# SwiGLU feed-forward in bf16: x turned by DMAs in a written order, and the last output tile in column pieces of 256, 128 and 128

## The chip, the core and the metric

The kernel runs on one core of one Trainium2 chip. The metric is device microseconds of one execution, given as the median of several runs. Engines are named as in the profile: PE is TensorE's matmuls and PEld its weight loads, DVE is VectorE, ACT ScalarE, POOL GpSimd, and SP the engine whose queue issues every DMA here. SBUF is the on-chip memory of 128 partitions; PSUM is the memory of eight banks for each partition that TensorE writes into.

## What is computed

```python
B, S, D, F = 32, 32, 512, 1792        # x (B,S,D), w1 and w3 (D,F), w2 (F,D), all bf16

gate = jnp.einsum("bsd,df->bsf", x, w1)
up   = jnp.einsum("bsd,df->bsf", x, w3)
h    = silu(gate) * up                # silu(g) = g * sigmoid(g)
out  = jnp.einsum("bsf,fd->bsd", h, w2)
```

B and S are flattened into N = 1024 tokens.

## The kernel before

With 128 partitions P, D is DT = 4 tiles, F is FT = 14 feature tiles, and N is NT = 8 token tiles or two blocks of NB = 512 tokens. A matmul contracts over the partition dimension, so the first stage needs x with features on partitions: that is `xT`, shaped (128, 4, 1024). It comes into being in two steps. Two DMAs load x with tokens on partitions into `x_sb` (lines 64 and 81). `x_transposes` (line 98) then turns each 128x128 piece on TensorE against an identity (`ident`, line 53), four pieces into one PSUM tile `pT` (line 103), and copies that tile to `xT`: on VectorE for block 0 (line 109), on ScalarE for block 1 (line 111).

All DMAs are issued by SP, in the order of lines 64 to 85: the first half of x, w1 and w3 in chunks of 2, 2, 2, 4 and 4 feature tiles (with the second half of x after the fourth pair of chunks), then w2 in two halves. Nine matmuls on a zeroed tile `warm_sb` keep TensorE at work during the first loads (line 90); POOL zeroes that tile (line 52).

Then, for each block of 512 tokens and each feature tile `fo`, TensorE makes a gate tile (4 matmuls of 128x512, line 119) and an up tile (4 more, line 127) in PSUM, two buffers each. ScalarE takes the sigmoid of the gate (line 135), VectorE multiplies gate by sigmoid (line 139) and the product by up (line 140), and writes bf16 into `hT`, which again has features on partitions.

In the second stage each token tile accumulates 14 matmuls of 128x512 over the feature tiles into `o_ps` (line 148); ScalarE casts it to bf16 (line 159) and SP stores it (line 160). The last token tile is made in two pieces of 256 columns, 14 matmuls each, and VectorE casts them (line 157).

The order in which each engine executes is not the written one: the framework's scheduler decides it from its own estimate. So the transposes of block 1, which the program writes after all of block 0, stand on TensorE among block 0's matmuls. PSUM's eight banks hold two buffers of `pT`, two each of gate and up, and two of `o_ps`.

Of the kernel before, what the change touches and what calls it, by code (L numbers as in the profile page):

```python
# [1 line left out]

# [5 lines left out]


@with_exitstack
def kernel(
    ctx: ExitStack,
    tc: tile.TileContext,
    x: bass.AP,
    w1: bass.AP,
    w3: bass.AP,
    w2: bass.AP,
    out: bass.AP,
):  # L20
    nc = tc.nc
    P = nc.NUM_PARTITIONS
    fp32 = mybir.dt.float32
    bf16 = mybir.dt.bfloat16

    B, S, D = x.shape
    F = w1.shape[1]
    N = B * S
    assert D % P == 0 and F % P == 0 and N % P == 0
    DT = D // P  # L30
    FT = F // P
    NT = N // P
    NB = 512
    assert N % NB == 0 and NB % P == 0
    NBLK = N // NB
    NT_PER_BLK = NB // P

    x_flat = x.flatten_outer_dims()
    out_flat = out.flatten_outer_dims()
    x_view = x_flat.rearrange("(nt p) d -> p nt d", p=P)  # L40
    w1_v = w1.rearrange("(dt p) f -> p dt f", p=P)
    w3_v = w3.rearrange("(dt p) f -> p dt f", p=P)
    w2_v = w2.rearrange("(ft p) d -> p ft d", p=P)

    consts = ctx.enter_context(tc.tile_pool(name="consts", bufs=1))
    work = ctx.enter_context(tc.tile_pool(name="work", bufs=3))
    psum_t = ctx.enter_context(tc.tile_pool(name="psum_t", bufs=2, space=bass.MemoryType.PSUM))
    psum = ctx.enter_context(tc.tile_pool(name="psum", bufs=2, space=bass.MemoryType.PSUM))
    psum2 = ctx.enter_context(tc.tile_pool(name="psum2", bufs=2, space=bass.MemoryType.PSUM))

    warm_sb = consts.tile([P, NB], bf16, name="warm_sb")
    nc.gpsimd.memset(warm_sb[:], 0.0)  # L52
    ident = consts.tile([P, P], bf16, name="ident")
    make_identity(nc, ident[:])

    x_sb = consts.tile([P, NT, D], bf16, name="x_sb")
    xT = consts.tile([P, DT, N], bf16, name="xT")
    w1_sb = consts.tile([P, DT, F], bf16, name="w1_sb")
    w3_sb = consts.tile([P, DT, F], bf16, name="w3_sb")
    w2_sb = consts.tile([P, FT, D], bf16, name="w2_sb")  # L60
    hT = consts.tile([P, FT, N], bf16, name="hT")

    half = NT // 2
    nc.sync.dma_start(out=x_sb[:, 0:half, :], in_=x_view[:, 0:half, :])  # L64

    chunk_sizes = [2, 2, 2, 4, 4]
    bounds = []
    cb = 0
    for csz in chunk_sizes:
        ce = min(FT, cb + csz)  # L70
        if cb < ce:
            bounds.append((cb, ce))
        cb = ce
    assert cb >= FT, (cb, FT)

    for i, (cb0, cb1) in enumerate(bounds):
        f0, f1 = cb0 * P, cb1 * P
        nc.sync.dma_start(out=w1_sb[:, :, f0:f1], in_=w1_v[:, :, f0:f1])  # L78
        nc.sync.dma_start(out=w3_sb[:, :, f0:f1], in_=w3_v[:, :, f0:f1])  # L79
        if i == 3:  # L80
            nc.sync.dma_start(out=x_sb[:, half:NT, :], in_=x_view[:, half:NT, :])

    FH = FT // 2
    nc.sync.dma_start(out=w2_sb[:, 0:FH, :], in_=w2_v[:, 0:FH, :])
    nc.sync.dma_start(out=w2_sb[:, FH:FT, :], in_=w2_v[:, FH:FT, :])

    NWARM = 9
    warm_ps = psum_t.tile([P, NB], fp32, name="warm_ps", tag="tp")
    for i in range(NWARM):
        nc.tensor.matmul(  # L90
            warm_ps[:],
            lhsT=warm_sb[:, 0:P],
            rhs=warm_sb[:],
            start=True,
            stop=True,
        )

    def x_transposes(nb: int):
        for dt in range(DT):
            pT = psum_t.tile([P, NB], bf16, name="pT", tag="tp")  # L100
            for j in range(NT_PER_BLK):
                nt = nb * NT_PER_BLK + j
                nc.tensor.transpose(  # L103
                    pT[:, j * P : (j + 1) * P],
                    x_sb[:, nt, dt * P : (dt + 1) * P],
                    ident[:],
                )
            if nb == 0:
                nc.vector.tensor_copy(xT[:, dt, nb * NB : (nb + 1) * NB], pT[:])  # L109
            else:  # L110
                nc.scalar.copy(xT[:, dt, nb * NB : (nb + 1) * NB], pT[:])  # L111

    for nb in range(NBLK):
        x_transposes(nb)
        for fo in range(FT):
            gate_ps = psum.tile([P, NB], fp32, name="gate_ps")
            up_ps = psum.tile([P, NB], fp32, name="up_ps")
            for dt in range(DT):
                nc.tensor.matmul(  # L119
                    gate_ps[:],  # L120
                    lhsT=w1_sb[:, dt, fo * P : (fo + 1) * P],
                    rhs=xT[:, dt, nb * NB : (nb + 1) * NB],
                    start=(dt == 0),
                    stop=(dt == DT - 1),
                )
            for dt in range(DT):
                nc.tensor.matmul(  # L127
                    up_ps[:],
                    lhsT=w3_sb[:, dt, fo * P : (fo + 1) * P],
                    rhs=xT[:, dt, nb * NB : (nb + 1) * NB],  # L130
                    start=(dt == 0),
                    stop=(dt == DT - 1),
                )
            sig = work.tile([P, NB], fp32, name="sig")
            nc.scalar.activation(  # L135
                sig[:], gate_ps[:], mybir.ActivationFunctionType.Sigmoid
            )
            t = work.tile([P, NB], fp32, name="t")
            nc.vector.tensor_mul(t[:], gate_ps[:], sig[:])  # L139
            nc.vector.tensor_mul(hT[:, fo, nb * NB : (nb + 1) * NB], t[:], up_ps[:])  # L140

    for nt in range(NT):
        DB = 256 if nt == NT - 1 else 512
        assert D % DB == 0
        for db in range(D // DB):
            o_ps = psum2.tile([P, DB], fp32, name="o_ps", tag="o_ps")
            for fo in range(FT):
                nc.tensor.matmul(  # L148
                    o_ps[:],
                    lhsT=hT[:, fo, nt * P : (nt + 1) * P],  # L150
                    rhs=w2_sb[:, fo, db * DB : (db + 1) * DB],
                    start=(fo == 0),
                    stop=(fo == FT - 1),
                )
            o_sb = work.tile([P, DB], bf16, name="o_sb", tag="o_sb")
            if nt == NT - 1:
                nc.vector.tensor_copy(o_sb[:], o_ps[:])  # L157
            else:
                nc.scalar.copy(o_sb[:], o_ps[:])  # L159
            nc.sync.dma_start(  # L160
                out=out_flat[nt * P : (nt + 1) * P, db * DB : (db + 1) * DB],
                in_=o_sb[:],
            )


# [1 line left out]
_INS = ['x', 'w1', 'w3', 'w2']  # L167
_OUTS = [((32, 32, 512), 'bfloat16')]


# [23 lines left out]
```

## Time and profile before

| | |
|---|---|
| median of 13 runs | 92.55 us (91.28 to 93.02) |
| the profiled execution's own time | 91.86 us |
| its span, first to last instruction | 90.1 us |
| busy in the span: PE, PEld, DVE, ACT, POOL | 80.3, 37.7, 40.8, 24.2, 1.2 us |
| mean granted TensorE clock | 0.981 |
| moved by DMA | 7.67 MB, of which 1.05 MB written |

The span is what the trace covers; the execution's time is 1.76 us longer. TensorE's busy time is no measure of its load, since matmuls overlap; a start-to-start distance in a full stretch is. "L119" is line 119 above. In rows of the chain and the timeline the first number is the start in us, the second the length.

### The profile page before, as it was taken

The page shows a single profiled execution, that of the slowest core. Times are in us where ns is not written, and L with a number is a line of the kernel's source. Part 1 is how long each engine was busy: PE and PEld are TensorE (multiplying, and loading weights), DVE is VectorE, ACT ScalarE, POOL GpSimd, SP SyncE. Part 2 cuts the span into 40 slices and gives each one's busy share as a digit, 9 for nine tenths or more (in the row PEclk, how much of TensorE's full clock was granted, in tenths as well). Part 3 has the DMA queues.
Part 4 walks back from the last instruction along what each step waited for, and adds up shares of the span by engine and source line. Part 5 has one row for each costly group of instructions (what it writes and reads, how often), then busy time and mean ns, then how long its engine had stood idle before and what let it go on. Part 6 is the DMA issues. An engine that isn't in the chain of part 4 may idle for free.

```text
span 90.1 us, 1022 instructions
## 1 busy us (share of the span) xinstructions
PE 80.3 (89%) x384; PEld 37.7 (42%) x391; DVE 40.8 (45%) x62; ACT 24.2 (27%) x40; POOL 1.2 (1%) x7
## 2 busy tenths in 40 slices
PE   4989603999999999999999999999999999999960
PEld 1354202334444444454444444444444444444750
DVE  0045530338778887726887887877600000000030
ACT  5002200222342243575243234224022022202200
POOL 5000000000000000000000000000000000000000
PEclk9999999579999999999999999999999999999999
DMA  0999999997000000000000000000001110111021
GB/s 20 331 281 305 338 349 348 348 349 242 0 7 0 0 0 0 0 0 0 0 0 4 7 0 0 0 0 4 0 16 42 58 58 6 60 58 58 0 87 29
DMA packets 9461, 7.67 MB, mean 85 GB/s; under 512 B 368, under 2 KB 9456, under 8 KB 9456
## 3 DMA queue, kind: packets, MB, share of 16 engines
q1 hardware_dynamic: 9456, 7.60, 27.4%
q8 instruction: 3, 0.05, 0.2%
q14 instruction: 2, 0.02, 0.1%
HBM read 6.55 MB, written 1.05 MB: 84 GB/s over the span
## 4 chain that ended last, share of the span: by engine, by line
PE 78%; DMA 8%; SPq 7%; ACT 2%; issue 1%; DVE 0%; DVEq 0%
PE o_ps L148 26%; PE up_ps L127 26%; PE gate_ps L119 25%; DMA x_sb<-in_x_dram 8%; SPq L79 3%; SPq L78 3%; ACT xT L111 2%; SPq L64 0%; DVE o_sb L157 0%; PE pT L103 0%; DVEq L157 0%
## 5 line engine op out<-in xcount | busy, mean ns | idle before, releaser
L119 PE MATMUL gate_ps<-xT,w_sb 128*128 128x512 bf16 x109 | 29.8, 388 | 0.3 <-ACT xT L111 0.2
L127 PE MATMUL up_ps<-xT,w_sb 128*128 128x512 bf16 x110 | 29.5, 386 | 0.3 <-issue 0.2
L135 ACT ACTIVATE sig<-gate_ps 128x512 f32<-128x512 f32 x28 | 16.7, 597 | 41.9 <-PE gate_ps L119 40.7
L139 DVE TENSOR_TENSOR t<-gate_ps,sig 128x512 f32<-128x512 f32 x28 | 19.4, 691 | 15.0 <-ACT sig L135 14.8
L148 PE MATMUL o_ps<-w_sb,hT 128*128 128x512 bf16 (+1 forms) x124 | 24.4, 355 | 0.1
L140 DVE TENSOR_TENSOR hT<-t,up_ps 128x512 bf16<-128x512 f32 x28 | 19.2, 687 | 3.8 <-PE up_ps L127 1.2
L148 PEld LDWEIGHTS <-hT 128*128 128x128 bf16 x126 | 12.3, 98 | 11.9
L127 PEld LDWEIGHTS <-w_sb 128*128 128x128 bf16 x112 | 11.1, 99 | 14.4 <-issue 2.0
L119 PEld LDWEIGHTS <-w_sb 128*128 128x128 bf16 x112 | 11.0, 100 | 12.8 <-issue 0.8
L157 DVE CAST o_sb<-o_ps 128x256 bf16<-128x256 f32 x2 | 0.8, 424 | 22.2 <-PE o_ps L148 22.2
L159 ACT CAST o_sb<-o_ps 128x512 bf16<-128x512 f32 x7 | 4.1, 586 | 17.5 <-PE o_ps L148 15.1
L103 PE MATMUL pT<-ident,x_sb 128*128 128x128 bf16 x32 | 3.1, 226 | 4.7 <-DMA x_sb<-in_x_dram 4.4
L103 PEld LDWEIGHTS <-x_sb 128*128 128x128 bf16 x32 | 2.4, 103 | 6.8 <-DMA x_sb<-in_x_dram 4.9
L90 PE MATMUL warm_ps<-warm_sb 128*128 128x512 bf16 x9 | 4.0, 631 | 1.3 <-POOL warm_sb L52 1.3
L109 DVE COPY xT<-pT 128x512 bf16<-128x512 bf16 x4 | 1.6, 423 | 5.8 <-PE pT L103 5.7
L90 PEld LDWEIGHTS <-warm_sb 128*128 128x128 bf16 x9 | 1.2, 143 | 3.2 <-issue 1.9
L111 ACT COPY xT<-pT 128x512 bf16<-128x512 bf16 x4 | 2.1, 588 | 0.4 <-PE pT L103 0.4
L135 ACT ACT_TABLE_LOAD x1 | 1.3, 1283 | 0.7 <-PEq L178 0.7
L52 POOL MEMSET warm_sb<- 128x512 bf16 x1 | 0.5, 524 | 0.3 <-POOLq L178 0.3
masks.py:199 POOL TENSOR_SCALAR_AFFINE_SELECT ident<-ident 128x128 bf16<-128x128 bf16 x1 | 0.3, 292 | 0.1
masks.py:197 POOL MEMSET ident<- 128x128 bf16 x1 | 0.2, 205 | 0.0
L178 POOL MEMSET const-float32-0.0<- 128x1 f32 x1 | 0.1, 98 | 0.2 <-issue 0.2
(3 smaller groups left out, 0.3 us busy)
## 6 DMA issues: line engine op xcount, KB each, us to landing
w_sb<-in_w_dram SPq DMA_DIRECT2D x4, 512.0 KB, 7.2
w_sb<-in_w_dram SPq DMA_DIRECT2D x2, 896.0 KB, 10.4
w_sb<-in_w_dram SPq DMA_DIRECT2D x6, 256.0 KB, 5.5
x_sb<-in_x_dram SPq DMA_DIRECT2D x2, 512.0 KB, 5.5
out_dram<-o_sb SPq DMA_DIRECT2D x7, 128.0 KB, 1.7
out_dram<-o_sb SPq DMA_DIRECT2D x2, 64.0 KB, 1.5
```

Of the source, the lines that this page charges most:

```text
L78: nc.sync.dma_start(out=w1_sb[:, :, f0:f1], in_=w1_v[:, :, f0:f1])
L79: nc.sync.dma_start(out=w3_sb[:, :, f0:f1], in_=w3_v[:, :, f0:f1])
L90: nc.tensor.matmul(warm_ps[:], lhsT=warm_sb[:, 0:P], rhs=warm_sb[:], start=True, stop=True,)
L103: nc.tensor.transpose(pT[:, j * P : (j + 1) * P], x_sb[:, nt, dt * P : (dt + 1) * P], ident[:],)
L111: nc.scalar.copy(xT[:, dt, nb * NB : (nb + 1) * NB], pT[:])
L119: nc.tensor.matmul(gate_ps[:], lhsT=w1_sb[:, dt, fo * P : (fo + 1) * P], rhs=xT[:, dt, nb * NB : (nb + 1) * NB], start=(dt == 0), stop=(dt ...
L127: nc.tensor.matmul(up_ps[:], lhsT=w3_sb[:, dt, fo * P : (fo + 1) * P], rhs=xT[:, dt, nb * NB : (nb + 1) * NB], start=(dt == 0), stop=(dt = ...
L135: nc.scalar.activation(sig[:], gate_ps[:], mybir.ActivationFunctionType.Sigmoid)
L139: nc.vector.tensor_mul(t[:], gate_ps[:], sig[:])
L140: nc.vector.tensor_mul(hT[:, fo, nb * NB : (nb + 1) * NB], t[:], up_ps[:])
L148: nc.tensor.matmul(o_ps[:], lhsT=hT[:, fo, nt * P : (nt + 1) * P], rhs=w2_sb[:, fo, db * DB : (db + 1) * DB], start=(fo == 0), stop=(fo == ...
L159: nc.scalar.copy(o_sb[:], o_ps[:])
```

## The change

The changed kernel switches the scheduler off (`manual_schedule`), so every engine executes in the order written. x is turned on its way in: three transposing DMAs (`dma_start_transpose`) write `xT` straight from memory, tokens 0 to 255, 256 to 511 and 512 to 1023. `x_sb`, `ident`, `pT`, the 32 transposes and the eight copies are gone, and with them the two PSUM buffers of `pT`; gate and up have three buffers each. The warm-up matmuls read a constant 1.0, broadcast, that the framework sets up before the program starts, instead of a tile that POOL zeroes. Feature tiles 0 and 1 of block 0 are made together and in half-width matmuls (128x256): first both gates and both ups for tokens 0 to 255, then the same for tokens 256 to 511, then both SwiGLU groups. The last token tile of the output is made in pieces of 256, 128 and 128 columns.

```diff
-    psum_t = ctx.enter_context(tc.tile_pool(name="psum_t", bufs=2, space=bass.MemoryType.PSUM))
-    psum = ctx.enter_context(tc.tile_pool(name="psum", bufs=2, space=bass.MemoryType.PSUM))
-    psum2 = ctx.enter_context(tc.tile_pool(name="psum2", bufs=2, space=bass.MemoryType.PSUM))
+    psum_o = ctx.enter_context(tc.tile_pool(name="psum_o", bufs=2, space=bass.MemoryType.PSUM))
+    psum = ctx.enter_context(tc.tile_pool(name="psum", bufs=3, space=bass.MemoryType.PSUM))
 
-    warm_sb = consts.tile([P, NB], bf16, name="warm_sb")
-    nc.gpsimd.memset(warm_sb[:], 0.0)
-    ident = consts.tile([P, P], bf16, name="ident")
-    make_identity(nc, ident[:])
+    ctx.enter_context(tc.manual_schedule())
...
-    half = NT // 2
-    nc.sync.dma_start(out=x_sb[:, 0:half, :], in_=x_view[:, 0:half, :])
+    def load_x_transposed(n0, n1):
+        nc.sync.dma_start_transpose(out=xT[:, :, n0:n1], in_=x_flat[n0:n1, :])
...
-    for i, (cb0, cb1) in enumerate(bounds):
-        f0, f1 = cb0 * P, cb1 * P
-        nc.sync.dma_start(out=w1_sb[:, :, f0:f1], in_=w1_v[:, :, f0:f1])
-        nc.sync.dma_start(out=w3_sb[:, :, f0:f1], in_=w3_v[:, :, f0:f1])
-        if i == 3:
-            nc.sync.dma_start(out=x_sb[:, half:NT, :], in_=x_view[:, half:NT, :])
...
+    def load_w(c0, c1):
+        load_w1(c0, c1)
+        load_w3(c0, c1)
+
+    load_x_transposed(0, HB)
+    load_w(0, 2)
+    load_x_transposed(HB, NB)
+    load_w(2, 4)
+    load_w(4, 6)
+    load_x_transposed(NB, N)
+    load_w(6, 10)
+    load_w(10, FT)
...
+    one = nc.const_aps.tensor(1.0, [P, 1], bf16)
+    warm_ps = psum_o.tile([P, NB], fp32, name="warm_ps", tag="o_ps")
...
-            lhsT=warm_sb[:, 0:P],
-            rhs=warm_sb[:],
+            lhsT=one.to_broadcast([P, P]),
+            rhs=one.to_broadcast([P, NB]),
...
-    def x_transposes(nb: int):
+    def project(ps, w_sb, fo, n0, n1, c0):
...
-            pT = psum_t.tile([P, NB], bf16, name="pT", tag="tp")
-            for j in range(NT_PER_BLK):
-                nt = nb * NT_PER_BLK + j
-                nc.tensor.transpose(
-                    pT[:, j * P : (j + 1) * P],
-                    x_sb[:, nt, dt * P : (dt + 1) * P],
-                    ident[:],
-                )
-            if nb == 0:
-                nc.vector.tensor_copy(xT[:, dt, nb * NB : (nb + 1) * NB], pT[:])
-            else:
-                nc.scalar.copy(xT[:, dt, nb * NB : (nb + 1) * NB], pT[:])
+            nc.tensor.matmul(
+                ps[:, c0 : c0 + n1 - n0],
+                lhsT=w_sb[:, dt, fo * P : (fo + 1) * P],
+                rhs=xT[:, dt, n0:n1],
+                start=(dt == 0),
+                stop=(dt == DT - 1),
+            )
+
+    def gate_up_tiles():
+        gate_ps = psum.tile([P, NB], fp32, name="gate_ps")
+        up_ps = psum.tile([P, NB], fp32, name="up_ps")
+        return gate_ps, up_ps
+
+    def swiglu(gate_ps, up_ps, fo, nb):
+        sig = work.tile([P, NB], fp32, name="sig")
+        nc.scalar.activation(sig[:], gate_ps[:], SIGMOID)
+        t = work.tile([P, NB], fp32, name="t")
+        nc.vector.tensor_mul(t[:], gate_ps[:], sig[:])
+        nc.vector.tensor_mul(hT[:, fo, nb * NB : (nb + 1) * NB], t[:], up_ps[:])
+
+    g0, u0 = gate_up_tiles()
+    g1, u1 = gate_up_tiles()
+    project(g0, w1_sb, 0, 0, HB, 0)
+    project(g1, w1_sb, 1, 0, HB, 0)
+    project(u0, w3_sb, 0, 0, HB, 0)
+    project(u1, w3_sb, 1, 0, HB, 0)
+    project(g0, w1_sb, 0, HB, NB, HB)
+    project(g1, w1_sb, 1, HB, NB, HB)
+    project(u0, w3_sb, 0, HB, NB, HB)
+    project(u1, w3_sb, 1, HB, NB, HB)
+    swiglu(g0, u0, 0, 0)
+    swiglu(g1, u1, 1, 0)
 
     for nb in range(NBLK):
...
-        for fo in range(FT):
-            gate_ps = psum.tile([P, NB], fp32, name="gate_ps")
-            up_ps = psum.tile([P, NB], fp32, name="up_ps")
...
+        for fo in range(2 if nb == 0 else 0, FT):
+            gate_ps, up_ps = gate_up_tiles()
+            project(gate_ps, w1_sb, fo, nb * NB, (nb + 1) * NB, 0)
+            project(up_ps, w3_sb, fo, nb * NB, (nb + 1) * NB, 0)
+            swiglu(gate_ps, up_ps, fo, nb)
...
-        DB = 256 if nt == NT - 1 else 512
-        assert D % DB == 0
-        for db in range(D // DB):
-            o_ps = psum2.tile([P, DB], fp32, name="o_ps", tag="o_ps")
+        last = nt == NT - 1
+        c0 = 0
+        for DB in (D // 2, D // 4, D // 4) if last else (D,):
+            o_ps = psum_o.tile([P, DB], fp32, name="o_ps", tag="o_ps")
...
-                    rhs=w2_sb[:, fo, db * DB : (db + 1) * DB],
+                    rhs=w2_sb[:, fo, c0 : c0 + DB],
...
-            if nt == NT - 1:
+            if last:
...
-                out=out_flat[nt * P : (nt + 1) * P, db * DB : (db + 1) * DB],
+                out=out_flat[nt * P : (nt + 1) * P, c0 : c0 + DB],
...
+            c0 += DB
...
```

SP's list of loads moves with it. Before (tiles `x_sb`, `w1_sb`, `w3_sb`; the number is the buffer's; the shape is partitions x pieces x elements):

```order
L64 DMA x_sb_77<-in_x_dram 128x4x512
L78 DMA w1_sb_79<-in_w1_dram 128x4x256
L79 DMA w3_sb_80<-in_w3_dram 128x4x256
...
L78 DMA w1_sb_79<-in_w1_dram 128x4x512
L79 DMA w3_sb_80<-in_w3_dram 128x4x512
L81 DMA x_sb_77<-in_x_dram 128x4x512
```

And now, on the same engine (a row's wait names the completion count of one of eight DMA lanes, `DMAHW0` to `DMAHW7`, which the transfers take in turn):

```order
L57 DMA_TRANSPOSE xT_69<-in_x_dram 128x4x256
L60 DMA w1_sb_70<-in_w1_dram 128x4x256
L63 DMA w3_sb_71<-in_w3_dram 128x4x256
L57 DMA_TRANSPOSE xT_69<-in_x_dram 128x4x256
L60 DMA w1_sb_70<-in_w1_dram 128x4x256
L63 DMA w3_sb_71<-in_w3_dram 128x4x256
L60 DMA w1_sb_70<-in_w1_dram 128x4x256
L63 DMA w3_sb_71<-in_w3_dram 128x4x256
L57 DMA_TRANSPOSE xT_69<-in_x_dram 128x4x512 [waits DMAHW0_49]
L60 DMA w1_sb_70<-in_w1_dram 128x4x512 [waits DMAHW1_49]
```

The second half of x stood behind the weights of tiles 6 to 9; its transposing DMA now stands ahead of them, and the first half is split around the first pair of weights.

On TensorE, before, two transposes of block 1 stood between the up tile of feature tile 1 and the gate tile of feature tile 2 (`x_sb` is x as loaded, `ident` the identity):

```order
L127 MATMUL up_ps_147<-xT_78,w3_sb_80 128x512
L103 LDWEIGHTS x_sb_77 [waits DMAHW1_49]
L103 MATMUL pT_341<-ident_72,x_sb_77 128x128 [waits PE_49]
L103 LDWEIGHTS x_sb_77
L103 MATMUL pT_341<-ident_72,x_sb_77 128x128
L119 LDWEIGHTS w1_sb_79 [waits DMAHW3_49]
L119 MATMUL gate_ps_161<-xT_78,w1_sb_79 128x512 [waits DVE_49]
```

At the same place now, and at the start (rows between left out):

```order
L85 MATMUL warm_ps_89<-const-bfloat16-1.0 128x512
L95 LDWEIGHTS w1_sb_70 [waits DMAHW1_49]
L95 MATMUL gate_ps_99<-xT_69,w1_sb_70 128x256 [waits DMAHW0_49]
...
L95 LDWEIGHTS w3_sb_71 [waits DMAHW2_49]
...
L95 MATMUL gate_ps_99<-xT_69,w1_sb_70 128x256 [waits DMAHW3_49]
...
L95 MATMUL up_ps_102<-xT_69,w3_sb_71 128x256
L95 LDWEIGHTS w1_sb_70 [waits DMAHW4_49]
L95 MATMUL gate_ps_145<-xT_69,w1_sb_70 128x512
```

The transposes are gone from it, and the waits left are for x and weights in the order in which SP issues them: lanes 0, 1 and 2 at the start, lane 3 (the second quarter of x) between the two halves of the first pair, lane 4 ahead of feature tile 2.

More of the change, by code (lines that the diff above doesn't have):

```diff
@@ L28 @@
     N = B * S
-    assert D % P == 0 and F % P == 0 and N % P == 0
+    NB = 512
+    HB = NB // 2
     DT = D // P
@@ L32 @@
     NT = N // P
-    NB = 512
-    assert N % NB == 0 and NB % P == 0
     NBLK = N // NB
     NT_PER_BLK = NB // P
+    assert D % P == 0 and F % P == 0 and N % NB == 0
     x_flat = x.flatten_outer_dims()
     out_flat = out.flatten_outer_dims()
-    x_view = x_flat.rearrange("(nt p) d -> p nt d", p=P)
     w1_v = w1.rearrange("(dt p) f -> p dt f", p=P)
@@ L46 @@
     work = ctx.enter_context(tc.tile_pool(name="work", bufs=3))
-    psum_t = ctx.enter_context(tc.tile_pool(name="psum_t", bufs=2, space=bass.MemoryType.PSUM))
-    psum = ctx.enter_context(tc.tile_pool(name="psum", bufs=2, space=bass.MemoryType.PSUM))
-    psum2 = ctx.enter_context(tc.tile_pool(name="psum2", bufs=2, space=bass.MemoryType.PSUM))
-    warm_sb = consts.tile([P, NB], bf16, name="warm_sb")
-    nc.gpsimd.memset(warm_sb[:], 0.0)
-    ident = consts.tile([P, P], bf16, name="ident")
-    make_identity(nc, ident[:])
-    x_sb = consts.tile([P, NT, D], bf16, name="x_sb")
+    psum_o = ctx.enter_context(tc.tile_pool(name="psum_o", bufs=2, space=bass.MemoryType.PSUM))
+    psum = ctx.enter_context(tc.tile_pool(name="psum", bufs=3, space=bass.MemoryType.PSUM))
+    ctx.enter_context(tc.manual_schedule())
     xT = consts.tile([P, DT, N], bf16, name="xT")
@@ L85 @@
     nc.sync.dma_start(out=w2_sb[:, FH:FT, :], in_=w2_v[:, FH:FT, :])
+    one = nc.const_aps.tensor(1.0, [P, 1], bf16)
+    warm_ps = psum_o.tile([P, NB], fp32, name="warm_ps", tag="o_ps")
     NWARM = 9
-    warm_ps = psum_t.tile([P, NB], fp32, name="warm_ps", tag="tp")
     for i in range(NWARM):
@@ L113 @@
-    for nb in range(NBLK):
-        x_transposes(nb)
-        for fo in range(FT):
-            gate_ps = psum.tile([P, NB], fp32, name="gate_ps")
-            up_ps = psum.tile([P, NB], fp32, name="up_ps")
[L118 to L140, printed above, removed]
```

17 lines of the change are left out of this document (6 added, 11 removed).

## The prediction

> **What bounds the kernel now.** I read the page's head and its forty slices first, for where TensorE is not full.
>
> ```profile
> span 90.1 us, 1022 instructions
> PE   4989603999999999999999999999999999999960
> PEclk9999999579999999999999999999999999999999
> GB/s 20 331 281 305 338 349 348 348 349 242 0 7 0 0 0 0 0 0 0 0 0 4 7 0 0 0 0 4 0 16 42 58 58 6 60 58 58 0 87 29
> ```
>
> A slice is 2.25 us. PE is full from slice 8 to the last two, so the end is set by TensorE's own work; what is not work lies in the first 20 us, at one crossing in the middle, and in the tail. The hole at slices 4 to 6 falls where the DMA engines still run at 348 GB/s: it waits for a transfer. The granted clock halves just behind it. The chain of waits names the transfer:
>
> ```profile
> 7.46 7.39 DMA x_sb<-in_x_dram
> 14.85 0.05 issue
> 14.89 0.29 PE pT L103 x2
> 15.18 1.98 PE gate_ps L119 x6
> ```
>
> The second half of x is the tenth transfer in SP's list. It is issued at 7.46 and lands at 14.85, and two transposes of block 1 on TensorE stand in front of block 0's third feature tile. I then cut the span at the holes (columns: length, busy time and count of PE, granted clock, DMA share, GB/s):
>
> ```profile
> 5.12:10.47 5.35, 4.99 (x33) 1.00 1.13 314
> 10.47:14.89 4.42, 0.00 (x0) 1.00 1.10 348
> 14.89:19.08 4.19, 3.96 (x13) 0.59 1.10 348
> 37.42:40.88 3.46, 3.25 (x25) 1.00 0.00 0
> 84.13:87.16 3.03, 2.98 (x28) 1.00 0.19 60
> 87.16:90.10 2.94, 0.00 (x0) 1.00 0.09 27
> ```
>
> TensorE idles 4.42 us, then runs 4.19 us at 0.59 of its clock. Busy time overstates a pipelined matmul, so I take prices from start to start, out of the chain and the timeline:
>
> ```profile
> 20.32 0.86 PE gate_ps L119 x4
> 63.33 8.42 PE o_ps L148 x39
> 37.42 0.50 PE L103 MATMUL pT<-ident,x_sb 128*128 128x128 bf16 x6
> L103 PE MATMUL pT<-ident,x_sb 128*128 128x128 bf16 x32 | 3.1, 226 | 4.7 <-DMA x_sb<-in_x_dram 4.4 <-DVE xT L109 0.3
> ```
>
> 512 columns: 8.42/39 = 0.216 us. 256 columns: 3.03/28 = 0.108 (the window from 84.13). 128 columns: six in 0.50, of which the last takes 0.22 alone, so (0.50 − 0.22)/5 = 0.056. The mathematics then costs 224 × 0.2158 + 98 × 0.2158 + 28 × 0.108 = 72.5 us, whatever the order. TensorE works from 5.12 to 87.16, 82.0 us. So 9.5 us of that stretch are not the reference's work.
>
> **What the change takes away.** All 32 transposes go: 32 × 0.056 = 1.79 us. In 5.12 to 10.47 stand 16 transposes (0.90) and 16 matmuls (3.45), 4.35 us of 5.35; the other 1.00 us is waiting for the copies of x out of PSUM, and goes. The idle 4.42 us goes. From 14.89 two transposes and 11 matmuls are 2.49 us of work in 4.19; the clock's 1.70 us goes with the idle time ahead of it, if no idle time takes its place. From 37.42, 14 transposes and 11 matmuls are 3.15 of 3.46; 0.31 goes with the copies on ScalarE. Together 1.79 + 1.00 + 4.42 + 1.70 + 0.31 = 9.22 us, nearly all of the 9.5; the remaining 0.3 us of small gaps I leave in.
>
> **What it adds: three transposing DMAs.** No row shows one, so I bound their price p, the time that the queue gives to one quarter of x (256 tokens, 256 KB). Either SP or the DMA engines may spend it; the transfers behind wait in both cases.
>
> ```profile
> q1 hardware_dynamic: 9456, 7.60, 27.4%
> w_sb<-in_w_dram SPq DMA_DIRECT2D x6, 256.0 KB, 5.5
> ```
>
> Low end: the plain rate, 256 KB at 348 GB/s, 0.75 us. (It can't be below that, as these bytes move either way.) High end: a packet costs 0.274 × 16 × 90.1/9456 = 0.042 us of an engine's time. If each of 256 rows is cut at the 128 columns that go to one set of partitions, a quarter is 1024 pieces, 64 for each engine, 2.7 us. The nearest row is a weight load of 256 KB in 512 pieces, 0.75 us, 0.0235 us a piece; 1024 such would be 1.5. I take p = 1.7, the middle of the ends, a little above that row because nothing here shows the turning itself.
>
> The Trainium skill disagrees with itself on this price. Advanced Engine Details and Errata, section X-Bar Transpose (TRN2), has transposing DMAs as fast as plain ones, 350 to 400 GB/s; the sum would be the low end's. VectorE: DVE Perf Modes, section The three transpose paths, gives 1309 ns for one 128x128 tile through the DMA against 390 ns on TensorE; were eight tiles of a quarter to run one after another, p would be an estimated 10.5 us, and the change a large loss (third rival). No run here has shown either so far.
>
> **When TensorE starts.** Landing times come from the first transfer and the start of the timeline:
>
> ```profile
> DMA to landing us min/median/max: 3.6/5.5/7.4
> ```
>
> This row is the view of tile x_sb: its first 512 KB, issued at 0.73, landed at 4.33. At 348 GB/s 1.5 us of that are data, so 2.1 us are fixed.
>
> ```profile
> 0.73 0.52 POOL L52 MEMSET warm_sb<- 128x512 bf16 x1 [0.29 <-POOLq L178]
> 0.73 0.43 SPq L64 DMA_DIRECT2D x_sb<-in_x_dram  x1
> 1.31 4.02 PE L90 MATMUL warm_ps<-warm_sb 128*128 128x512 bf16 x9 [1.31 <-POOL warm_sb L52]
> 5.12 0.75 PE L103 MATMUL pT<-ident,x_sb 128*128 128x128 bf16 x8
> ```
>
> The warm-up no longer waits for a memset: it begins near 0.8 instead of 1.31 and, 3.81 us later, is over by 4.6. That brings nothing by itself, since the transfers come later: x quarter 0 lands at 0.73 + 2.1 + 1.7 = 4.53, w1 of tiles 0 and 1 at 5.28, where the first matmul starts: 0.16 us later than 5.12. Then w3 at 6.03, x quarter 1 at 7.73, w1 and w3 of tiles 2 and 3 at 8.48 and 9.23, of 4 and 5 at 9.98 and 10.73, the large transpose (3.4) at 14.13, w1 and w3 of tiles 6 to 9 at 15.63 and 17.13.
>
> TensorE needs: eight half-width gate matmuls, 0.86 us, then w3 at 6.15: there. Eight more, then quarter 1 at 7.01: it comes at 7.73, **a wait of 0.72 us**. Sixteen more, tile 2 at 9.46: there. Tiles 2 to 5 take 4 × 1.73, so w1 of tile 6 is needed at 16.4 (there at 15.63) and its w3 at 17.2 (there at 17.13, with nothing to spare). Block 1 needs the large transpose at 30, long landed. SP lets the ninth transfer, the large transpose, go only when the first has landed (4.53), about when SP gets there; behind it in SP's list stand the weights of tiles 6 to 13 and w2, and w2 isn't used before 54.
>
> **The pair at the start and PSUM.** Two SwiGLU groups now arrive together.
>
> ```profile
> L139 DVE TENSOR_TENSOR t<-gate_ps,sig 128x512 f32<-128x512 f32 x28 | 19.4, 691 | 15.0 <-ACT sig L135 14.8
> L140 DVE TENSOR_TENSOR hT<-t,up_ps 128x512 bf16<-128x512 f32 x28 | 19.2, 687 | 3.8 <-PE up_ps L127 1.2
> L135 ACT ACTIVATE sig<-gate_ps 128x512 f32<-128x512 f32 x28 | 16.7, 597 | 41.9 <-PE gate_ps L119 40.7 <-PE up_ps L127 1.1
> ```
>
> VectorE has 2 × 1.38 us to do after 0.60 for the first sigmoid. With three PSUM pairs tile 2 needs no release; tile 3 begins 1.73 us later, when the first gate has been free for 0.4 us (0.60 + 0.69 = 1.29), and its up part at 2.59, when the first pair has been free since 1.98. Hidden, at no cost; with only two pairs tile 2 would have waited 1.3 us. After that 1.38 us of VectorE a tile lies below TensorE's 1.73.
>
> **The last token tile.** The second 256-column piece becomes two of 128.
>
> ```profile
> 82.59 4.53 PE o_ps L148 x34
> 87.20 0.42 DVE o_sb L157
> out_dram<-o_sb SPq DMA_DIRECT2D x7, 128.0 KB, 1.7
> out_dram<-o_sb SPq DMA_DIRECT2D x2, 64.0 KB, 1.5
> ```
>
> On TensorE 14 × 0.108 = 1.51 becomes 28 × 0.056 = 1.57, no change. (Bound: if a weight load of 0.098 set the pace, +1.2 us; the transposes, one load each too, went at 0.056, so I take that.) After the last matmul: the 128x512 product takes 0.69 and the 128x256 cast 0.42, 1.05 ns a column, so a 128-column cast takes 0.29, 0.13 less; and 32 KB should land about 0.1 us sooner, as 64 KB does against 128 KB. The middle piece's cast and store fit beside the last piece's 0.78 us of matmuls. Tail −0.24.
>
> **Sum.** 90.1 − 9.22 + 0.16 + 0.72 − 0.24 = 81.5 us of span. The profiled execution took 91.86 us around its span of 90.1, so 1.76 lies outside: 83.3. That execution was 0.69 below the median of 92.55; against the median I forecast **84.0 us**. With p = 0.75 the start is 4.65 and no wait is left: 90.1 − 9.22 − 0.47 − 0.24 = 80.2, or 82.6 on the median. With p = 2.7 the start is 6.28 (+1.16), and waits of 1.72 (quarter 1), 1.27 and 0.64 (tile 6) appear: 85.4, or 87.9.
>
> **Rivals.** First, the clock. TensorE idles from 4.6 to 5.28 and for 0.72 again. The trace shows the clock falling after 4.42 idle us and staying up through pauses of 0.3, and nothing between. If such a pause is enough, one slow stretch costs 1.70 as before: 85.7. Second, the queue at the high end, p between 2 and 3.4: fewer waits are removed than new ones made ahead of quarter 1 and tile 6; 87.9. For it: every byte of the start passes one queue, already full for 20 us. Against it: the plain rate holds at 348 GB/s for pieces of 512 bytes.
>
> Third, the other side: the transposing queue is slow outright. Past p = 2 each further us costs four: one at the start, one ahead of quarter 1, two for the large transpose ahead of tile 6's weights. At p = 4 the sum is 90.1 − 9.22 + 2.46 + 7.53 − 0.24 = 90.6, or 93.1, so about p = 3.9 (67 GB/s) decides. Pieces four times smaller than at the high end, 64 bytes, would make p 10.8: start 14.38, waits 9.82, 17.47 and 0.64, and **120 us**. (Element by element, 131,072 packets a quarter, it would be over 1000.) For it: these words are scattered to another layout, and no row shows the machine doing that. Against it: only the lack of evidence.
>
> **How the numbers follow.** Forecast 0.53, clock 0.13, second rival 0.20, p above 3.4 0.14. The first three are faster by over 1%, about what a measurement of this kernel can tell from no change: 0.86. Of the last 0.04 lies near p = 3.9, within 1%, and 0.10 is slower. The range runs from 82.3, a little under the low end, to 90.0, which takes in the clock, the high end of p and both together (89.6), and leaves out most of the last case.
>
> **What would show it.** Right: no DMA wait of TensorE above 1 us; first real matmul near 5.3; granted clock at 1.00 from then on; quarter 1's landing about 0.7 us behind its need; no gap near 35 to 40 us; PE's end near 78.8, with 2.7 us behind it. Wrong: the issues of the transposes or their landings lasting several us, idle time ahead of quarter 1 or tile 6, a clock under 0.9 in the first 20 us, or the last 28 matmuls taking 2.7 us.

## The result, and the profile after

The changed kernel takes 83.44 us, median of 11 runs (82.94 to 85.07), against 92.3 for the kernel before (48 runs): a ratio of 0.9098, 95% interval 0.9065 to 0.9132. The forecast was 84.0. Four of these eleven runs, at 84.7 to 85.1 us, and some further down, one of them at 140.32, count as disturbed, and the ratios leave such runs out, so a median over all runs can lie above what its ratio says. The profiled execution took 83.18 us with a span of 81.4.

The head of the page, after:

```profile
span 81.4 us, 1010 instructions
PE   6949999999999999999999999999999999999960
GB/s 0 162 281 247 293 246 200 373 352 350 351 341 33 0 0 0 0 0 0 0 4 0 8 0 0 0 0 0 0 64 64 8 56 64 13 63 64 21 89 19
```

The hole is gone, and TensorE is full from slice 3 on; the loads last until about 24.5 us instead of 22, with a first stretch that moves less (a slice is 2.04 us). The start, in the timeline (start, length, engine, line, work; in brackets the idle time before, and what ended it):

```profile
0.73 1.32 SPq L57 DMA_TRANSPOSE xT<-in_x_dram  x1
2.10 0.57 SPq L60 DMA_DIRECT2D w_sb<-in_w_dram  x1
2.74 0.49 SPq L63 DMA_DIRECT2D w_sb<-in_w_dram  x1
3.27 1.49 SPq L57 DMA_TRANSPOSE xT<-in_x_dram  x1
...
5.86 1.05 PE L95 MATMUL gate_ps<-xT,w_sb 128*128 128x256 bf16 x8 [1.09 <-DMA w_sb<-in_w_dram]
...
7.08 4.19 SPq L57 DMA_TRANSPOSE xT<-in_x_dram  x1
```

TensorE idles 1.09 us after the warm-up and begins at 5.86, when w1 lands, 0.58 later than forecast. A transposing DMA holds SP for 1.3 to 4.2 us, where these plain ones take 0.5 to 0.6. From 5.86 to the end, cut where the stages change (length, busy time and count, granted clock, DMA share, GB/s):

```profile
5.86:9.36 3.50, 3.50 (x32) 1.00 1.14 253
9.36:53.50 44.14, 43.93 (x203) 1.00 0.38 110
53.50:75.73 22.23, 22.12 (x104) 1.00 0.11 36
75.73:78.76 3.03, 3.01 (x42) 1.00 0.18 60
78.76:81.40 2.64, 0.00 (x0) 1.00 0.13 30
```

TensorE works 72.9 us in one piece, against the 72.5 that the mathematics costs. The last token tile still takes 3.03 us, with 42 matmuls instead of 28, and the tail is 2.64 instead of 2.94. TensorE's stretch from its first real matmul to its last shrank from 82.04 us to 72.90. The span's difference closes by the forecast's own terms: 90.1 − 9.22 (removed) + 0.74 (start at 5.86 instead of 5.12) + 0.08 (a wait at feature tile 6) − 0.30 (tail) = 81.4. That wait is a piece of the chain, four matmuls in 0.94 instead of 0.86:

```profile
17.30 0.94 PE up_ps L95 x4
```

### The profile page after: what moved, and what is told of

It reads as the page before. It is cut to its first block, busy times and chain, and to the rows that moved or that the text cites. A ratio compares the mean times of both kernels' runs of the same rounds, so it can differ in the third digit from the quotient of the medians.

```text
span 81.4 us, 1010 instructions
## 1 busy us (share of the span) xinstructions
PE 76.6 (94%) x383; PEld 37.1 (46%) x389; DVE 39.3 (48%) x59; ACT 22.0 (27%) x36; POOL 0.2 (0%) x4
## 2 busy tenths in 40 slices
DMA packets 12741, 7.67 MB, mean 94 GB/s; under 512 B 4800, under 2 KB 12736, under 8 KB 12736
## 3 DMA queue, kind: packets, MB, share of 16 engines
HBM read 5.51 MB, written 1.05 MB: 81 GB/s over the span
## 4 chain that ended last, share of the span: by engine, by line
PE 89%; DMA 5%; SPq 2%; issue 1%; DVE 0%; DVEq 0%
PE gate_ps L95 30%; PE up_ps L95 30%; PE o_ps L141 30%; DMA w_sb<-in_w_dram 5%; SPq L57 2%; DVE o_sb L150 0%; DVEq L150 0%
## 5 line engine op out<-in xcount | busy, mean ns | idle before, releaser
L95 PEld LDWEIGHTS <-w_sb 128*128 128x128 bf16 x240 | 23.3, 98 | 26.8 <-DMA w_sb<-in_w_dram 2.4
L95 PE MATMUL gate_ps<-xT,w_sb 128*128 128x512 bf16 (+1 forms) x118 | 28.5, 365 | 1.2 <-DMA w_sb<-in_w_dram 1.1
L95 PE MATMUL up_ps<-xT,w_sb 128*128 128x512 bf16 (+1 forms) x118 | 28.5, 365 | 0.1
L141 PE MATMUL o_ps<-w_sb,hT 128*128 128x512 bf16 (+2 forms) x138 | 24.3, 336 | 0.1
L150 DVE CAST o_sb<-o_ps 128x128 bf16<-128x128 f32 (+1 forms) x3 | 1.0, 336 | 22.3 <-PE o_ps L141 22.3
L85 PE MATMUL warm_ps<-const-bfloat16-1.0 128*128 128x512 bf16 x9 | 4.0, 629 | 0.8 <-PEq L172 0.8
L85 PEld LDWEIGHTS <-const-bfloat16-1.0 128*128 128x128 bf16 x9 | 1.2, 141 | 2.7 <-issue 2.7
```

Of the source, the lines that this page charges most:

```text
L85: nc.tensor.matmul(warm_ps[:], lhsT=one.to_broadcast([P, P]), rhs=one.to_broadcast([P, NB]), start=True, stop=True,)
L95: nc.tensor.matmul(ps[:, c0 : c0 + n1 - n0], lhsT=w_sb[:, dt, fo * P : (fo + 1) * P], rhs=xT[:, dt, n0:n1], start=(dt == 0), stop=(dt == D ...
L141: nc.tensor.matmul(o_ps[:], lhsT=hT[:, fo, nt * P : (nt + 1) * P], rhs=w2_sb[:, fo, c0 : c0 + DB], start=(fo == 0), stop=(fo == FT - 1),)
```

## The experiments

The theory after the result: of the 9.2 us removed, 6.1 were the late second half of x and the half clock behind it, which is a matter of order; the rest are the transposes and copies; and the transposing DMAs cost the start 0.7 us. The rival: the gain is that of turning x outside TensorE.

**One load moved in the kernel before.**

```diff
-        if i == 3:
+        if i == 1:
             nc.sync.dma_start(out=x_sb[:, half:NT, :], in_=x_view[:, half:NT, :])
```

> The kernel before with one line moved: the second half of x is loaded after the second pair of weight chunks instead of after the fourth. The order on TensorE is unchanged, all transposes and copies stay. Theory (two thirds of the 9.2 us removed were the late load and the clock behind it, 4.42 + 1.70): x lands near 8.9, before its need at 10.5, the idle stretch and the half clock are gone, about 86.2 us (92.3 - 6.1), span near 84. Rival (the gain came from TensorE being rid of its 32 transposes and their copies, and a stall removed here only turns up elsewhere): above 90 us.

Measured: 86.04 us, ratio 0.9361 (0.9288 to 0.9435). The same three windows as before the change:

```profile
5.12:10.47 5.35, 4.59 (x28) 1.00 1.04 300
10.47:14.89 4.42, 4.15 (x20) 1.00 1.09 340
14.89:19.08 4.19, 4.19 (x21) 1.00 1.10 349
```

Where TensorE idled 4.42 us it now works, and the clock of the next window is 1.00 instead of 0.59. One moved line, with every transpose still on TensorE, brings 6.4 of the change's 8.9 us of median. x landed later than expected, though:

```profile
3.40 7.24 DMA x_sb<-in_x_dram
10.64 0.05 issue
10.68 0.28 PE pT L103 x2
```

10.64, not 8.9: TensorE waited half a microsecond for it.

**The scheduler off, nothing else.**

```diff
+    ctx.enter_context(tc.manual_schedule())
     warm_sb = consts.tile([P, NB], bf16, name="warm_sb")
```

> The kernel before with the scheduler off, nothing else: all of block 1's transposes stand behind block 0's matmuls, the loads as before. Theory: the idle 4.42 us and the clock's 1.70 go as well, since nothing needs the second half of x before 30 us; but 16 transposes now wait for four copies on ScalarE in a row (4 x 0.59 + 0.2 = 2.6 us, of which 0.9 is the transposes), against 1.1 us above the matmuls before: about 1 us is given back, 87.2 us. Rival (the gain is the transposing DMAs'): above 90 us.

Measured: 86.31 us, ratio 0.9371 (0.93 to 0.9442). The same gain by the opposite means: the load stays late, and what needs it is late too. The price is at the crossing between the blocks:

```profile
31.19:34.01 2.82, 2.19 (x20) 1.00 0.00 0
```

16 transposes and four gate matmuls are 1.76 us of work in 2.82; 1.06 is lost there to the copies, against 0.31 before. The theory stands. 2.6 to 2.9 us of the change are left for what its other parts bring together: no transposes, no copies, the pair at the start and the tail. But for the tail (below), no run here takes these apart.

**What the turning costs at the start: plain loads in its place.**

```diff
-        nc.sync.dma_start_transpose(out=xT[:, :, n0:n1], in_=x_flat[n0:n1, :])
+        r = (n1 - n0) // P
+        v = x_flat[n0:n1, :].rearrange("(p r) (c e) -> p (r c) e", r=r, c=4 // r)
+        nc.sync.dma_start(out=xT[:, :, n0:n1], in_=v)
```

> The changed kernel with the three transposing DMAs replaced by plain loads of the same bytes into the same tile, in pieces of 512 and 1024 bytes: x is not turned, so the output is not the reference's. All else, and every wait, is the same. Theory (the start is set by what the turning costs the queue, 1.3 us or more a quarter against 0.75 and 0.5 us of SP's time): w1 is issued near 1.25 and lands near 4.9, the first matmul starts there instead of at 5.86, the wait ahead of tile 6 is gone: 0.9 to 1.2 us faster, 82.4 us. Rival (5.86 is set by the weights' own transit): 83.4 within 0.2.

Measured: 83.25 us, ratio 0.9058 (0.9011 to 0.9106). The rival is right about the time, and the theory about the first matmul:

```profile
4.90 1.88 PE L97 MATMUL gate_ps<-xT,w_sb 128*128 128x256 bf16 x8
6.90 1.05 PE L97 MATMUL up_ps<-xT,w_sb 128*128 128x256 bf16 x8
```

```profile
2.07 4.79 DMA w_sb<-in_w_dram
6.85 0.04 issue
6.90 1.05 PE up_ps L97 x8
```

The gates begin at 4.90 as the theory had it, but the up matmuls can't start before w3, which takes 4.79 us from its issue and lands at 6.85. In the changed kernel w3 is issued 0.67 us later, lands 3.8 after that, near 6.6, and the up matmuls start at 6.74. This run alone does not show that w3 holds the start, since its eight gate matmuls go at half rate here (1.88 us instead of 1.05) and are over only at about 6.8; the next run does, with gates at full rate. Behind w3 the second half's gates need quarter 1. Its landing is the median of the three loads of x, counted from the issue, first in the changed kernel (issued at 3.27), then here (issued at 2.61):

```profile
DMA to landing us min/median/max: 3.3/4.3/6.1
```

```profile
DMA to landing us min/median/max: 3.3/5.1/6.0
```

That is 7.6 with the turning and 7.7 without, and the second half's gates start at 7.62 and 7.78. So the 0.7 us at the start are not saved by plain loads: the data of the first pair is complete no sooner.

**w1 ahead of the first transposing DMA.**

```diff
-    load_x_transposed(0, HB)
-    load_w(0, 2)
+    load_w1(0, 2)
+    load_x_transposed(0, HB)
+    load_w3(0, 2)
```

> The changed kernel with w1 of tiles 0 and 1 issued ahead of the first transposing DMA, w3 behind it. Theory: w1 lands near 4.3, x quarter 0 near 5.0, so the first matmul starts near 5.0 and not at 5.86; but w3 is still issued at 2.7 and lands near 6.5, which the up matmuls then wait for: of 0.86 us 0.4 stay, 83.0 us. Rival (plain transfers in flight slow the turning down, as they did with the weights on the other queue, where quarter 0 landed at 6.66): the first matmul is no earlier than 5.8, and the time is 83.4 or more.

Measured: 83.4 us, ratio 0.9071 (0.9015 to 0.9128).

```profile
4.71 1.03 PE L96 MATMUL gate_ps<-xT,w_sb 128*128 128x256 bf16 x8 [0.24 <-DMA xT<-in_x_dram]
6.48 1.05 PE L96 MATMUL up_ps<-xT,w_sb 128*128 128x256 bf16 x8 [0.73 <-DMA w_sb<-in_w_dram]
7.51 1.03 PE L96 MATMUL gate_ps<-xT,w_sb 128*128 128x256 bf16 x8
```

The first matmul is 1.15 us earlier, the up matmuls stand until w3 lands at 6.43, and the gates of the second half start at 7.51, only 0.11 earlier than in the change (7.62). The ups themselves started 0.26 earlier; the rest went into a wait for quarter 1, which lands near 7.5 here (issued at 3.21):

```profile
DMA to landing us min/median/max: 3.4/4.3/6.1
```

So w3 and, right behind it, quarter 1 hold the start, and the expected 0.4 us did not show in the median.

**The first weights on ScalarE's queue.**

```diff
     load_x_transposed(0, HB)
-    load_w(0, 2)
+    nc.scalar.dma_start(out=w1_sb[:, :, 0 : 2 * P], in_=w1_v[:, :, 0 : 2 * P])
+    nc.scalar.dma_start(out=w3_sb[:, :, 0 : 2 * P], in_=w3_v[:, :, 0 : 2 * P])
```

> The changed kernel with w1 and w3 of feature tiles 0 and 1 issued by ScalarE's queue instead of SP's, at the same time as SP issues the first transposing DMA. Theory (the first matmul is late, 5.86, because SP is held 1.32 us by the transposing DMA and issues w1 only at 2.10; the DMA engines are not full then): w1 is issued near 0.75, lands near 4.5, the first matmul starts when the warm-up ends, near 4.8; about 1.0 us faster, 82.4 us. Rival (the DMA engines themselves are held by the transposing): w1 still lands near 5.8 and the time stays at 83.4 within 0.3.

Measured: 83.68 us, ratio 0.9087 (0.9013 to 0.9162): no gain, the rival. But not as the rival had it:

```profile
4.55 0.10 PEld L96 LDWEIGHTS <-w_sb 128*128 128x128 bf16 x1 [0.69 <-DMA w_sb<-in_w_dram]
...
6.70 1.05 PE L96 MATMUL gate_ps<-xT,w_sb 128*128 128x256 bf16 x8 [2.17 <-DMA xT<-in_x_dram]
7.57 1.89 PE L96 MATMUL up_ps<-xT,w_sb 128*128 128x256 bf16 x8
```

The profile is of an execution of 85.6 us, so it shows the order of the landings and not what the median is made of: behind the pause of 2.17 us the up matmuls ran at half rate, 1.89 us for eight. w1 did land near 4.5. Now x is late: the quarter that took 3.3 us alone lands 5.9 us after its issue, when two plain loads go beside it on another queue. So, in this profile, the start is not short of SP's time alone; the transfers slow one another.

**What one more quarter costs later on.** First with the warm-up as it is, then with 13 warm-up matmuls.

```diff
     load_x_transposed(NB, N)
+    x_dummy = consts.tile([P, DT, HB], bf16, name="x_dummy")
+    nc.sync.dma_start_transpose(out=x_dummy[:], in_=x_flat[0:HB, :])
     load_w(6, 10)
```

> The changed kernel with one more transposing DMA, of 256 tokens into a tile that nobody reads, ahead of the weights of feature tiles 6 to 9. Theory (no slack is left at that place, the w3 of tile 6 is waited for by some hundredths of a us already, and one quarter costs the queue 1.3 to 2.1 us): a wait of 1.3 to 2.1 us ahead of tile 6, 85.0 us. Rival (the turning only holds SP, while the data engines have enough queued): 83.4 within 0.3.

Measured: 85.18 us, ratio 0.9268 (0.9216 to 0.932). The time is the expected one, but the profile does not show the expected cause:

```profile
4.18:6.13 1.95, 0.01 (x2) 1.00 1.35 277
7.10:10.60 3.50, 3.50 (x20) 0.55 1.19 288
```

In this execution TensorE idled 1.95 us ahead of its first real matmul, and the clock then fell to 0.55 for some 3.5 us. That made TensorE late at tile 6 and hid the wait there. So the run is inconclusive by itself, and was repeated without the pause (`NWARM = 13`).

> The run with one more transposing DMA of 256 tokens ahead of the weights of tiles 6 to 9, now with 13 warm-up matmuls, so that no pause precedes the first real matmul. Theory (a quarter costs the queue 1.3 to 2.1 us, and there is next to no slack at tile 6; in the first run the slow clock made TensorE late enough to hide it): the clock stays up and a wait of 1 to 2 us stands ahead of tile 6; 84.9 us. Rival (the time of the first run was the clock's alone, and the turning costs nothing here): 83.4 within 0.3.

Measured: 85.16 us, ratio 0.9231 (0.9175 to 0.9286).

```profile
17.67 1.04 PE L97 MATMUL gate_ps<-xT,w_sb 128*128 128x512 bf16 x4 [0.91 <-DMA w_sb<-in_w_dram]
19.29 1.04 PE L97 MATMUL up_ps<-xT,w_sb 128*128 128x512 bf16 x4 [0.58 <-DMA w_sb<-in_w_dram]
```

The run with 13 warm-up matmuls and no extra quarter (below) has the same two groups here:

```profile
16.44 1.03 PE L95 MATMUL gate_ps<-xT,w_sb 128*128 128x512 bf16 x4
17.30 1.03 PE L95 MATMUL up_ps<-xT,w_sb 128*128 128x512 bf16 x4
```

Tile 6's up matmuls come 1.99 us later, and the kernel takes 1.8 us more than that run's 83.36. One quarter of x costs about 1.8 to 2.0 us where no slack is left. By landings it is 1.9 to 2.3: w3 of tiles 6 to 9 lands at 19.15 and 19.25 in the two runs with the extra quarter, and between 16.98 and 17.25 in the five kept profiles that have the same order of loads there and no such quarter.

**The pause and the clock.** `NWARM = 9` became 13, and in another run 4.

> The changed kernel with 13 warm-up matmuls instead of 9, so that TensorE has work through the 1.09 us before its first real matmul. Theory (a pause of that length does not lower the clock, and the start is set by a transfer): the same within 0.3 us of 83.4, granted clock 1.00. Rival (the pause costs clock later): faster by up to 1 us; if the four are run at half rate, 0.5 us slower.

> The changed kernel with 4 warm-up matmuls instead of 9: TensorE pauses from about 2.5 us until the weights land at 5.9. Theory (a pause of about 2 us or more lowers the clock, as in the run with the extra transposing DMA, where 1.95 us idle were followed by 3.5 us at 0.55; one of 1.09 us did not in the profile of the change): the first 3 us of real matmuls go at half rate, 1.5 to 1.8 us slower, 85.0 us. Rival (the clock falls only for pauses near 4 us, as in the kernel before): within 0.3 us of 83.4.

Measured: 83.36 us with 13, ratio 0.9072 (0.9018 to 0.9126), and 85.46 us with 4, ratio 0.9228 (0.9153 to 0.9302). With 4, in the timeline and then the chain of waits:

```profile
6.04 1.89 PE L95 MATMUL gate_ps<-xT,w_sb 128*128 128x256 bf16 x8 [3.41 <-DMA w_sb<-in_w_dram]
```

```profile
6.04 1.89 PE gate_ps L95 x8
7.93 1.71 PE up_ps L95 x8
9.63 1.30 PE gate_ps L95 x8
10.94 0.87 PE up_ps L95 x8
```

Eight matmuls of 256 columns take 1.71 us there, 0.214 each, and 0.87 later, 0.109 each: half rate until about 10. Both times came out as the theory said, the slow one a little more than it: the change's own pause of 1.09 us cost nothing in its profile, and having only 4 warm-up matmuls cost 2.0 us. The theory's reason is not shown by that run, though. Its four warm-up matmuls were at half rate too (1.86 us), so the full rate may have come late rather than been lost in the pause. A loss is shown where matmuls ran at full rate before it: with the extra quarter, and with the weights on ScalarE's queue, they did so for 0.8 to 0.9 us behind pauses of 1.95 and 2.17 us, and then went at half rate. The six runs with 13 lie between 83.27 and 83.56 us, closer together than the change's; no kept trace shows whether its pause is behind that.

**The last tile in two pieces again.**

```diff
-        for DB in (D // 2, D // 4, D // 4) if last else (D,):
+        for DB in (D // 2, D // 2) if last else (D,):
```

> The changed kernel with the last token tile in two pieces of 256 columns again. Theory: the tail is 0.24 us longer, 83.7 us against 83.44. Rival (weight loads of 0.098 us pace the 128-column matmuls): three pieces cost TensorE 1.2 us, and two pieces are 1.0 us faster, 82.4.

Measured: 84.73 us, ratio 0.9123 (0.9045 to 0.9201), against 0.9098: by the ratios 0.23 us slower, well inside the intervals, so the time alone does not decide between the theory and no effect. The rival's 1.0 us faster would be a ratio near 0.899, below this interval. In the profile the last cast is 0.42 us again instead of 0.29, and its tail is 81.8 − 78.9 = 2.9 instead of 2.64.

```profile
78.89 0.03 DVEq L150
78.92 0.04 issue
78.97 0.42 DVE o_sb L150
```

**A version out of these.** w1 first, the third transposing DMA behind the weights of tiles 6 to 9, and 11 warm-up matmuls.

> The changed kernel with w1 of tiles 0 and 1 issued first, the third transposing DMA moved behind the weights of tiles 6 to 9, and 11 warm-up matmuls. Theory (the first up matmul waits for w3, which lands between 6.4 and 6.9 in every order so far; the wait ahead of tile 6 goes; no pause for the clock): 83.0 us, at most 0.5 faster than the change. Rival (the first matmul's time sets the end): first matmul near 4.8, 82.4.

Measured: 83.12 us, ratio 0.9013 (0.896 to 0.9066). The up matmuls again waited, 0.83 us, for w3, and tile 2 waited 0.35 for its w1. At 0.3 us below the change's median, and with intervals that meet, it is not shown to be faster.

## Why the prediction was right

The forecast of 84.0 us met 83.44, and its span of 81.5 met 81.4. By its steps:

- **What bounds the kernel**: right. One transfer in front of TensorE's list cost 4.42 + 1.70 us; moving either the transfer or what needs it brings these back (86.04 and 86.31 against an expected 86.2 and 87.2).
- **What goes away, 9.22 us**: right as a sum, which closes to 81.4 with the measured rest; 6.1 of it by two experiments, the transposes and copies only as what is left.
- **p = 1.7 us a quarter**: close, where the queue is full: the extra quarter cost 1.8 to 2.0 us. At the start the turning cost nothing against plain loads, with quarter 1 there at 7.6 against 7.7. With the extra quarter packets rose by 1056 (12741 to 13797), 1024 of which fit the pieces of 256 bytes that the high end assumed. As 256 KB in 1.8 us this is 146 GB/s. The Trainium skill's page Advanced Engine Details and Errata, section X-Bar Transpose (TRN2), has the turning as fast as a plain load, 350 to 400 GB/s; this trace does not agree. The Trainium skill's page VectorE: DVE Perf Modes, section The three transpose paths, gives 1309 ns a tile; eight one after another would be an estimated 10.5 us, so it would fit only as the time of one tile while others overlap it, which no run here shows.
- **The start**: right within its sum, wrong in its parts. Forecast 0.16 for a later first matmul and 0.72 for quarter 1; measured 0.74 and nothing, with 0.08 at tile 6. The step that failed is the train of landings, "w1 of tiles 0 and 1 at 5.28": it put all of p behind one fixed 2.1 us, but SP is held 1.32 us by the transposing DMA and issues w1 at 2.10. Quarter 1 was put at 7.73 and landed near 7.6, and the later first matmul took away the wait for it. Two errors of 0.6 us cancel, so that the start's sum came out is luck. Of the forecast's own signs three were missed: the first real matmul near 5.3, no wait above 1 us (1.09), and quarter 1 late by 0.7 us. One sign of its being wrong appeared, an issue of 4.19 us, with no wait behind it but the 0.08 at tile 6.
- **The start as a cost of turning**: plain loads, and w1 ahead of x, showed that it is not. w3 lands between 6.4 and 6.9 in every kept profile of the change and its variants, and quarter 1 between 7.3 and 7.9; the ups of the first half and the gates of the second can't begin sooner. In the kernel before w3 landed at 6.7 (issued at 1.76, 4.9 later); in its two variants, with the same first three loads, at 6.2 and 7.3, so one order alone scatters by a microsecond.
- **The clock as a rival**: a pause short of 4.42 us can lower it, 1.95 us did. The change's profile escaped it with 1.09 us; whether all its executions did is open.
- **The other side**, p above 3.9: not so. **The pair at the start and PSUM**: no wait there. **The last tile**: 3.03 us on TensorE as forecast (3.08), the tail −0.30 for −0.24.

What stays open: what makes w3 take 3.6 to 5.6 us to land; how much of the remaining 2.6 to 2.9 us each of the change's other parts brings; and whether smaller first weights would let the start pass.

## What to carry to other kernels

When a stall has a transfer's name on it, first ask why the waiting instruction stands so early or the transfer so late: a single moved line gave 6.4 of the 8.9 us here, and it also gave back the clock. Count a start by all the bytes that the first full group of matmuls needs, not by the first matmul; bringing that one forward by 1.15 us brought nothing. And fill a pause at the start with idle matmuls up to the landing: with 13 instead of 9 it cost nothing here, and with 4 the kernel took 2.0 us more.

## What the hardware showed beside this

A transposing DMA holds SP's queue far longer than a plain one, 1.23 to 2.30 us for 256 tokens against 0.56 and 0.64, and 3.63 to 5.43 us for 512 tokens against 0.66. With plain loads on another queue it landed 5.9 us after its issue instead of 3.3. The record of the granted clock does not show the half rate of a start: the window of the nine warm-up matmuls reads

```profile
0.77:4.77 4.00, 4.00 (x9) 1.00 0.56 136
```

while these 512-column matmuls start 0.43 us apart, twice the 0.216 of later ones: the distance from start to start tells. The moment at which full rate began differed by execution: with the extra quarter two of the nine warm-up matmuls were already 0.22 apart, at 3.58 and 3.80; with plain loads the gates from 4.90 to 6.8 were still at half rate; and with 13 warm-up matmuls only the last, at 5.82, was at full rate, so that the chain shows 5.44 us for them:

```profile
0.77 5.44 PE warm_ps L85 x13
```
